# Float32 weights on SyncE's queue with a cast on chip, more chunks singly through the FFN, fewer transposes on TensorE

## The chip, the cores and the metric

One Trainium2 chip; the kernel runs on one of its cores. A core has TensorE (PE, matrix multiply, with its weight loads shown apart as PEld), VectorE (DVE), ScalarE (ACT), GpSimd (POOL) and SyncE (SP, which here only issues transfers), and 16 DMA engines that all queues share. The metric is the device time of one execution in microseconds (us).

## The reference

The kernel is a linear-attention layer followed by a feed-forward network (FFN). For each of 4 batches and 8 heads (head size 48) it walks 768 positions with a state of 48 x 48:

```
cur   = outer(u * k_t, v_t)
y_t   = r_t . (state + cur)
state = w * state + outer(k_t, v_t)
```

The 8 heads of y, side by side, make 384 columns; all batches make 3072 rows x. Then

```
h   = max(x @ w_in, 0)        # w_in  384 x 2048
out = (h * h) @ w_out         # w_out 2048 x 384
```

Inputs and output are float32; the kernel multiplies in bf16.

## The kernel before, in words

The 3072 positions are cut into 24 chunks of 128: chunk i is batch i % 4, block i // 4 of its 768 positions. Within a chunk the recurrence becomes matrix work; from block to block a state per batch is carried. The kernel's steps have short names, each with a number of its chunk, and one function `do_<name>` each:

- L: three loads of k, r, v of one chunk (192 KB each, in pieces of 192 bytes), on SP's queue (L482).
- kh, rt: k and r times powers of w, written as bf16 into `rk` (L496, L499). P0, P, du, dv: the term of u, as products, a row sum and a product (L503, L507, L511, L520). vb: v as bf16, on ACT (L525).
- Tk, Tr: transposes of kh and rt by TensorE (L531), evicted from PSUM as ek and er (L491 on ACT, L493 on DVE). From chunk PE_T on, T takes their place: one DMA transpose on SP's queue (L552).
- A, M: k times r (L562), masked on DVE (L576). Y: masked product times v, plus r times the state (L588, L593). U, S: the state's update (L603, L617, L618).
- xs: Y + dv (L611). X, xT: its transpose on TensorE (L624) and the copy to SBUF on ACT (L632).
- W1_q, W2_q: a quarter each of w_in and w_out, loaded on POOL's software queue, which casts float32 to bf16 on the way (L638, L643).
- F: a slice of the first FFN product into one PSUM bank (L652). R: relu on ACT (L665). Q: the square, on DVE (L674) or, for each fourth slice, on ACT (L672). G: a quarter of the second product (L684). os, st: eviction and store (L695, L699).

The FFN takes chunks singly or in pairs: `units()` makes the first SINGLE_HEAD and the last SINGLE_TAIL chunks single, the rest pairs. A single chunk has 4 F slices of 12 matmuls with 128 columns; a pair has 8 slices of 6 matmuls with 256.

The order on each engine isn't written out by hand. `Plan` holds every step with its possible engines, a cost on each, its needs and a priority (about a due time, one chunk each 6.25 us); `run()` places the steps one by one where they can start first, with a small model of the two DMA queues, and the instructions are issued in that order. Engines and SP's queue work in order: an instruction that waits holds all behind it. The model has room for 8 PSUM banks. `after` names a transfer's extra waits in the program: W1_q waits for v of chunk 1, W2_q for k or v of chunks 3 and 4. `OPEN` shifts the priorities of the first four chunks' steps, FLEX is the number of first chunks whose products may go to DVE as well as POOL, UB is the priority of u's row, SLACK adds time in the plan between a step and its reader, and LEAD places the loads of a chunk behind the T of an earlier one.

Of the kernel before, what the change touches and what calls it, by code (L numbers as in the profile page):

```python
# [8 lines left out]
FP32 = mybir.dt.float32  # L9
BF16 = mybir.dt.bfloat16  # L10
# [186 lines left out]
def make_plan():  # L197
    p = Plan()
    P = PERIOD
# [12 lines left out]
    all_units = units()  # L212
    unit_of = {i: n for n, chunks in enumerate(all_units) for i in chunks}

    def parts(n):
        return 4 * len(all_units[n])

    for i in range(N):
# [51 lines left out]
        p.add(f"xs{i}", "DVE", 0.47, [f"Y{i}", f"dv{i}"] + ([f"X{i-3}"] if i >= 3 else []), prio=t + 2.5,  # L270
              lat=0.65, give=[f"Y{i}"])
# [3 lines left out]
        p.add(f"X{i}", "PE", 0.17, [f"xs{i}"], prio=t + 3.0, lat=0.4, take=(f"X{i}", "A", 1), slack=SLACK[1] if i >= 4 else 0.0)  # L275
        p.add(f"xT{i}", "ACT", 0.38, [f"X{i}"] + ([f"F{n-4}_{parts(n-4)-1}"] if n >= 4 else []), prio=t + 3.0,
              lat=0.6, give=[f"X{i}"])
    for q in range(4):
        p.add(f"W1_{q}", "POOL", 0.85, W1GATE[q], prio=-60 + q, service=2.3)
        p.after[f"W1_{q}"] = W1GATE[q]  # L280
    for q in range(4):
        p.add(f"W2_{q}", "POOL", 0.85, W2GATE[q], prio=-55 + q, service=2.4)
        p.after[f"W2_{q}"] = W2GATE[q]
    for n, chunks in enumerate(all_units):
        i0, size = chunks[0], len(chunks)
        for s in range(parts(n)):
            t = (i0 / 2 + 1) * P + s * P / 8
            q = s // size
            p.add(f"F{n}_{s}", "PE", 0.66, [f"xT{i}" for i in chunks] + [f"W1_{q}"], prio=t, lat=0.95,
                  take=(f"H{n}_{s}", "H", 1))  # L290
            on_act = s % 4 == 3
            p.add(f"R{n}_{s}", "ACT", 0.49, [f"F{n}_{s}"], prio=t, lat=0.7,
                  give=[f"H{n}_{s}"] if on_act else [])
            p.add(f"Q{n}_{s}", "ACT" if on_act else "DVE", 0.53 if on_act else 0.6,
                  [f"R{n}_{s}"], prio=t + 0.7, lat=0.8, give=[] if on_act else [f"H{n}_{s}"],
                  ring=("hq", HQ, [f"G{i}_{q}" for i in chunks]))
        for j, i in enumerate(chunks):
            for q in range(4):
                t = (i0 / 2 + 2) * P + (4 * j + q) * P / 8
                p.add(f"G{i}_{q}", "PE", 0.65,  # L300
                      [f"Q{n}_{size*q+a}" for a in range(size)] + [f"W2_{q}"] + ([f"G{i}_{q-1}"] if q else []),
                      prio=t + 0.3, lat=0.95, take=(f"O{i}", "O", 1) if q == 0 else ())
# [7 lines left out]
def kernel(  # L310
# [11 lines left out]
    nc = tc.nc  # L322
# [13 lines left out]
    loads = ctx.enter_context(tc.tile_pool(name="loads", bufs=8))  # L336
    work = ctx.enter_context(tc.tile_pool(name="work", bufs=4))
    hid = ctx.enter_context(tc.tile_pool(name="hid", bufs=HQ))
    psum = ctx.enter_context(tc.tile_pool(name="psum", bufs=1, space=bass.MemoryType.PSUM))

    plan = make_plan()
# [284 lines left out]

    def do_xT(i):
        n = unit_of[i]
        j = all_units[n].index(i)
        if n not in xTs:  # L630
            xTs[n] = work.tile([128, CCH, GT], BF16, name=f"xT_{n}", tag="xT")
        nc.scalar.copy(xTs[n][:, :, L * j : L * (j + 1)], ps.pop(f"X{i}"))  # L632

    def do_W1(q):
        n = d_ff // 4
        t = const.tile([128, CCH, n], BF16, name=f"W1_{q}")
        W1[q] = t
        return nc.gpsimd.dma_start(out=t, in_=w_in_t[:, :, n * q : n * (q + 1)])  # L638

    def do_W2(q):  # L640
        t = const.tile([128, 4, d_model], BF16, name=f"W2_{q}")
        W2[q] = t
        return nc.gpsimd.dma_start(out=t, in_=w_out_t[:, 4 * q : 4 * q + 4, :])  # L643

    def do_F(n, s):
        size = len(all_units[n])
        per, wide = 4 // size, L * size
        hp = bank(f"H{n}_{s}").rearrange("p (a t) -> p a t", a=per)
        for fi in range(per):
            f = (per * s + fi) % 4  # L650
            for c in range(CCH):
                nc.tensor.matmul(  # L652
                    hp[:, fi, :],
                    W1[s // size][:, c, 128 * f : 128 * (f + 1)],
                    xTs[n][:, c, 0:wide],
                    start=(c == 0),
                    stop=(c == CCH - 1),
                    skip_group_check=True,
# [53 lines left out]
    for key in order:  # L712
        if key in plain:
            inst = plain[key]()
        elif key[:2] in ("W1", "W2"):
            inst = (do_W1 if key[1] == "1" else do_W2)(int(key[3:]))
        elif key[0] == "L":
            inst = do_L(key[1], int(key[2:]))
        elif "_" in key:
# [39 lines left out]
```

## Time and profile before

| | us |
|---|---|
| median of 3 runs (range) | 178.98 (178.73 to 179.65) |
| the profiled execution | 178.95 |
| its span, first to last instruction | 177.2 |
| PE busy | 165.6 (93%) |
| DVE busy | 132.2 (75%) |
| POOL busy | 110.3 (62%) |
| ACT busy | 107.0 (60%) |

Busy time counts an instruction from start to end. A matmul that waits for its operands, or whose neighbours do, looks long, so a busy PE early in the kernel isn't a PE at work all the time. The clock granted to TensorE was 0.997 of full speed. The DMA share is the mean over 16 engines and can go over 1, since packets of one engine overlap. Times in rows count from the start of the span.

### The profile page before, as it was taken

To read this page: it belongs to the slowest core of one execution; us is meant where nothing else is said; L and a number is where in the kernel's file an instruction comes from. 1 tells how busy PE (TensorE), PEld (TensorE's weight loads), DVE (VectorE), ACT (ScalarE), POOL (GpSimd) and SP (SyncE) were. 2 spreads that over 40 slices of the span, in tenths; PEclk is the share of its full clock that TensorE was granted. 3 is DMA by queue.
4 is the path that set the end of the run, shared out by engine and by line. 5 is a ranking of instruction groups with operands and counts; after the bars stand their busy time and mean duration, and the time that the engine had idled before them with its cause. 6 is when DMAs were issued, how large, how long until landed. Compare 5 with 4: busy or idle time off the path is not lost.

```text
span 177.2 us, 4677 instructions
## 1 busy us (share of the span) xinstructions
PE 165.6 (93%) x1852; PEld 126.6 (71%) x1852; DVE 132.2 (75%) x235; ACT 107.0 (60%) x208; POOL 110.3 (62%) x130
## 2 busy tenths in 40 slices
PE   2779789999999999999999999999999999999991
PEld 1249668787878886687786876877777777778750
DVE  4699999876789986499799879797796566544400
ACT  4444468747776766377386676576756654655622
POOL 5299416959988889999799968998694000000000
PEclk9999999999999999999999999999999999999998
DMA  3999999998999684879999999899794011110112
GB/s 75 202 177 200 191 185 185 186 210 160 202 203 218 174 159 83 158 150 253 185 175 213 117 216 225 174 227 197 149 183 128 0 48 44 44 41 7 44 46 89
DMA packets 97913, 26.25 MB, mean 148 GB/s; under 512 B 91234, under 2 KB 97892, under 8 KB 97892
## 3 DMA queue, kind: packets, MB, share of 16 engines
q1 hardware_dynamic: 94180, 22.82, 68.3%
q0 software_dynamic: 3712, 3.15, 11.1%
q8 instruction: 14, 0.23, 0.6%
q14 instruction: 7, 0.06, 0.1%
HBM read 20.45 MB, written 4.72 MB: 142 GB/s over the span
## 4 chain that ended last, share of the span: by engine, by line
PE 83%; DVE 9%; DMA 2%; issue 2%; SPq 1%; ACT 0%; DVEq 0%
PE ps_O L684 36%; PE ps_H L652 34%; PE ps_A L562 4%; PE ps_Y L593 2%; PE ps_X L624 2%; PE ps_Y L588 2%; DMA rf<-in_r_dram 2%; PE ps_U L603 2%; DVE dv L520 2%; DVE Bm L576 2%; DVE rk L499 1%; PE ps_Tr L531 1%; DVE hq L674 1%; DVE du L511 1%; PE ps_Tk L531 1%
## 5 line engine op out<-in xcount | busy, mean ns | idle before, releaser
L665 ACT ACTIVATE hr<-ps_H 128x512 bf16<-128x512 f32 x96 | 56.4, 598 | 34.5 <-PE ps_H L652 31.4
L652 PE MATMUL ps_H<-xT,W 128*128 128x128 bf16 (+1 forms) x768 | 76.1, 247 | 0.1
L684 PE MATMUL ps_O<-W,hq 128*128 128x384 bf16 x384 | 73.4, 326 | 0.0
L652 PEld LDWEIGHTS <-W 128*128 128x128 bf16 x768 | 59.1, 98 | 8.8 <-issue 0.2
L674 DVE TENSOR_TENSOR hq<-hr,ps_H 128x512 bf16<-128x512 bf16 x72 | 47.1, 681 | 13.3 <-ACT hr L665 13.3
L684 PEld LDWEIGHTS <-hq 128*128 128x128 bf16 x384 | 35.2, 98 | 17.3
L576 DVE TENSOR_TENSOR Bm<-ps_A,maskJT 128x512 bf16<-128x512 f32 x48 | 30.8, 683 | 12.2 <-PE ps_A L562 12.1
L496 POOL TENSOR_TENSOR rk<-kf,Wkhat 128x384 bf16<-128x384 f32 x23 | 23.6, 1024 | 8.1 <-DMA kf<-in_k_dram 6.9
L507 POOL TENSOR_TENSOR P<-P,ub 128x384 f32<-128x384 f32 x22 | 22.0, 1001 | 5.4 <-DVE P L503 5.2
L499 POOL TENSOR_TENSOR rk<-rf,Wt 128x384 bf16<-128x384 f32 x21 | 21.0, 1001 | 3.8 <-ACT hr L665 2.4
L503 POOL TENSOR_TENSOR P<-rf,kf 128x384 f32<-128x384 f32 x22 | 22.3, 1014 | 0.0
L520 POOL TENSOR_TENSOR dv<-vf,du 128x384 f32<-128x384 f32 x20 | 16.6, 830 | 6.9 <-DVE du L511 5.8
L632 ACT COPY xT<-ps_X 128x384 bf16<-128x384 bf16 x24 | 11.5, 478 | 10.3 <-PE ps_X L624 10.3
L525 ACT CAST vb<-vf 128x384 bf16<-128x384 f32 x24 | 12.2, 510 | 7.0 <-DMA vf<-in_v_dram 7.0
L672 ACT ACTIVATE hq<-hr 128x512 bf16<-128x512 bf16 x24 | 15.3, 635 | 0.1
L611 DVE TENSOR_TENSOR xs<-ps_Y,dv 128x384 bf16<-128x384 f32 x24 | 13.3, 552 | 1.9 <-PE ps_Y L593 1.8
L695 ACT COPY os<-ps_O 128x384 f32<-128x384 f32 x24 | 11.4, 477 | 4.4 <-PE ps_O L684 4.1
L511 DVE TENSOR_REDUCE du<-P 128x8 f32<-128x384 f32 x24 | 13.0, 544 | 0.7 <-POOL P L507 0.7
L593 PE MATMUL ps_Y<-vb,Bm 128*128 128x48 bf16 x192 | 11.9, 186 | 0.2
L618 DVE TENSOR_TENSOR S0W<-ps_U,WLm 128x384 bf16<-128x384 f32 x20 | 11.0, 556 | 0.6
L593 PEld LDWEIGHTS <-Bm 128*128 128x128 bf16 x192 | 10.0, 98 | 1.5 <-DVE Bm L576 0.5
L562 PE MATMUL ps_A<-rkT 48*128 48x128 bf16 x192 | 10.2, 229 | 0.7 <-ACT rkT L491 0.7
(52 smaller groups left out, 116.3 us busy)
## 6 DMA issues: line engine op xcount, KB each, us to landing
kf<-in_k_dram SPq DMA_DIRECT2D x24, 192.0 KB, 4.5
rf<-in_r_dram SPq DMA_DIRECT2D x24, 192.0 KB, 4.5
vf<-in_v_dram SPq DMA_DIRECT2D x24, 192.0 KB, 4.6
out_dram<-os SPq DMA_DIRECT2D x24, 192.0 KB, 2.5
W<-in_moe_w_in_dram POOLq DMA_DIRECT2D x4, 384.0 KB, 9.3
W<-in_moe_w_out_dram POOLq DMA_DIRECT2D x4, 384.0 KB, 8.3
rkT<-rk SPq DMA_TRANSPOSE x15, 3.4
wrow<-in_w_dram SPq DMA_DIRECT2D x1, 1.5 KB
```

The costliest lines, as they stand in the source:

```text
L496: engine(f"kh{i}").tensor_mul(rk_buf[i % NK][:, 1, :, 0:D], nat["k", i], Wkhat)
L499: engine(f"rt{i}").tensor_mul(rk_buf[i % NK][:, 0, :, 0:D], nat["r", i], Wt2)
L503: engine(f"P0{i}").tensor_mul(P0, nat["r", i], nat["k", i])
L507: engine(f"P{i}").tensor_mul(P0s[i], P0s[i], ub)
L520: engine(f"dv{i}").tensor_mul(dv, nat["v", i], du_b)
L562: nc.tensor.matmul(Ap[e][:, hc, :], rkT[p0 : p0 + D, HP + hc, :], rkT[p0 : p0 + D, hc, :], start=True, stop=True, skip_group_check=True,)
L576: nc.vector.tensor_mul(Bm[:, e], Ap[e], mask_b)
L593: nc.tensor.matmul(Y[:, hc, D * e : D * (e + 1)], Bm[:, e, hc, :], vb[:, 2 * hc + e, :], start=(c == 0), stop=True, skip_group_check=True,)
L652: nc.tensor.matmul(hp[:, fi, :], W1[s // size][:, c, 128 * f : 128 * (f + 1)], xTs[n][:, c, 0:wide], start=(c == 0), stop=(c == CCH - 1), ...
L665: nc.scalar.activation(hr, hp, AF.Relu)
L674: nc.vector.tensor_mul(hq, hr, hp)
L684: nc.tensor.matmul(ps[f"O{i}"][:, 0:d_model], hsq[n, f // per][:, f % per, L * j : L * (j + 1)], W2[q][:, f % 4, :], start=(f == 0), stop= ...
```

## The change

Constants:

```diff
-PE_T = 9
+PE_T = 6
-SINGLE_HEAD = 8
-SINGLE_TAIL = 0
+SINGLE_HEAD = 10
+SINGLE_TAIL = 2
-FLEX = 4
-UB = -94.95
-ST_SLACK = 3.0
+FLEX = 5
+UB = -94.75
+ST_SLACK = 2.0
-W2GATE = [["Lk3"], ["Lk3"], ["Lv3"], ["Lv4"]]
-LEAD = 3
-SLACK = (2.5, 0.5)
-LGATE = {}
-OPEN = {"kh": 8, "rt": -3, "P0": 8, "P": -3, "du": 0.0, "dv": 0.0, "S": 0.0}
+W2GATE = [["Lv3"], ["Lk4"], ["Lv4"], ["Lk5"]]
+HW1 = (0, 1, 2, 3)
+HW2 = (0, 1, 2)
+W1PRIO = (-93.5, -93.45, -92.4, -92.35)
+W2PRIO = (-91.5, -91.4, -91.3, -91.2)
+CASTS = ("ACT", "POOL")
+XD = 24
+WF = 5
+LEAD = 2
+SLACK = (1.0, 0.6, 0.5)
+LGATE = {6: ["W2_2"], 7: ["W2_3"]}
+OPEN = {"kh": 0, "rt": 12, "P0": -6, "P": 2, "du": 8, "dv": 0, "S": 2}
```

All four quarters of w_in and the first three of w_out are loaded as float32 by SP's queue into one of WF = 5 staging tiles, between the loads of the first chunks (loads of chunk i have priority -95 + i there), and a new step C casts each on ACT or POOL, whichever the plan finds free first. F and G wait for C instead of W. The last quarter of w_out stays on POOL's queue, and waits for k of chunk 5. The loads of chunk 6 wait in the program for W2_2, those of chunk 7 for W2_3. With XD = 24 no chunk takes the new path by which xT could be a DMA transpose.

```diff
+        for q in range(4):
+            if q in hw:
+                p.add(f"W{a}_{q}", "SP", 0.7, prio=prios[q], service=hw_time, ring=("wf", WF, [f"C{a}_{q}"]))
+                p.add(f"C{a}_{q}", CASTS, {e: {"ACT": 1.33, "POOL": 1.9, "DVE": 1.6}[e] for e in CASTS},
+                      [f"W{a}_{q}"], prio=-30 + q)
+            else:
+                p.add(f"W{a}_{q}", "POOL", 0.85, gates[q], prio=-60 + q, service=sw_time)
+                p.after[f"W{a}_{q}"] = gates[q]
...
+    def do_W(a, q):
+        part, shape = w_of[a](q)
+        if plan.eng[f"W{a}_{q}"] == "SP":
+            Wf[a, q] = stage.tile(shape, FP32, name=f"Wf{a}_{q}", tag="Wf")
+            return nc.sync.dma_start(out=Wf[a, q], in_=part)
+        Wb[a][q] = const.tile(shape, BF16, name=f"W{a}_{q}")
+        return nc.gpsimd.dma_start(out=Wb[a][q], in_=part)
+
+    def do_C(a, q):
+        f = Wf.pop((a, q))
+        Wb[a][q] = const.tile(list(f.shape), BF16, name=f"W{a}_{q}")
+        copy(f"C{a}_{q}", Wb[a][q], f)
```

xT is laid out chunk by chunk, so that a pair's F reads two blocks of 128 columns instead of 256 in a row:

```diff
-            xTs[n] = work.tile([128, CCH, GT], BF16, name=f"xT_{n}", tag="xT")
-        nc.scalar.copy(xTs[n][:, :, L * j : L * (j + 1)], ps.pop(f"X{i}"))
+            xTs[n] = work.tile([128, size, CCH, L], BF16, name=f"xT_{n}", tag="xT", padded_shape=[None, 2, None, None])
+        nc.scalar.copy(xTs[n][:, j], ps.pop(f"X{i}"))
...
-                    xTs[n][:, c, 0:wide],
+                    xTs[n][:, :, c, :],
```

More of the change, by code (lines that the diff above doesn't have):

```diff
@@ L274, in make_plan, with ready_of @@
                   lat=1.2 if c else 0.65, give=[f"U{i}"])
[L275 to L283, printed above, removed]
+        room = [f"F{n-4}_{parts(n-4)-1}"] if n >= 4 else []
+        if i < XD:
+            p.add(f"X{i}", "PE", 0.17, [f"xs{i}"], prio=t + 3.0, lat=0.4, take=(f"X{i}", "A", 1),
+                  slack=SLACK[1] if i >= 4 else 0.0)
+            p.add(f"xT{i}", "ACT", 0.38, [f"X{i}"] + room, prio=t + 3.0, lat=0.6, give=[f"X{i}"])
+        else:
+            p.add(f"xT{i}", "SP", 0.9, [f"xs{i}"] + room, prio=t + 3.0, service=0.6, slack=SLACK[2])
+    for a, hw, gates, prios, hw_time, sw_time in (
+        (1, HW1, W1GATE, W1PRIO, 2.05, 2.3), (2, HW2, W2GATE, W2PRIO, 2.1, 2.4)
+    ):
+        for q in range(4):
[3 more added lines that the diff above has]
+                      [f"W{a}_{q}"], prio=-30 + q)
+            else:
+                p.add(f"W{a}_{q}", "POOL", 0.85, gates[q], prio=-60 + q, service=sw_time)
+                p.after[f"W{a}_{q}"] = gates[q]
+    def ready_of(a, q):
+        return f"C{a}_{q}" if q in (HW1 if a == 1 else HW2) else f"W{a}_{q}"
     for n, chunks in enumerate(all_units):
@@ L288, in make_plan @@
             q = s // size
[L289 removed]
+            p.add(f"F{n}_{s}", "PE", 0.66, [f"xT{i}" for i in chunks] + [ready_of(1, q)], prio=t, lat=0.95,
                   take=(f"H{n}_{s}", "H", 1))
```

31 lines of the change are left out of this document (16 added, 15 removed).

## The prediction

> **What bounds the kernel now.** I read the page's slices first, then busy time by stretch, then the head in order of time.
>
> ```profile
> span 177.2 us, 4677 instructions
> PE   2779789999999999999999999999999999999991
> DVE  4699999876789986499799879797796566544400
> DMA  3999999998999684879999999899794011110112
> ```
>
> ```profile
> 3.54:16.66 13.12, 10.62 (x74) 7.24 (x75) 10.57 (x18) 5.34 (x12) 8.57 (x9) 1.00 1.18 190
> 16.66:26.36 9.70, 7.88 (x122) 6.86 (x118) 9.65 (x16) 5.07 (x10) 3.61 (x5) 1.00 1.23 188
> 28.16:173.40 145.24, 145.24 (x1634) 110.72 (x1631) 108.44 (x191) 92.76 (x183) 95.60 (x103) 1.00 0.76 145
> 173.40:177.30 3.90, 0.07 (x1) 0.00 (x0) 0.00 (x0) 0.48 (x1) 0.00 (x0) 0.87 0.28 101
> ```
>
> In the second fence a row gives a stretch, its length, then busy time (and instructions) of PE, weight loads, DVE, ACT and POOL, the clock, the DMA share and GB/s. From 28.16 to 173.40 us TensorE has no gap: 145.24 of 145.24 us. After it come 3.8 us of last eviction and store. So the span is a head of 28.2 us, a solid block, and a tail, and an edit pays in two ways only: it takes matmul work out of the block, or it gets more of that work done before the block begins. A third way loses: a supplier of the block comes so late that a gap opens. In the head TensorE looks 80% busy, but 74 instructions in 10.62 us are matmuls stretched by waiting; the full engines there are DVE (9.65 of 9.70 us) and the DMA (share 1.18 to 1.23, about 190 GB/s, against 0.76 later).
>
> ```profile
> 5.85 0.56 DVE L503 TENSOR_TENSOR P<-rf,kf 128x384 f32<-128x384 f32 x1 [2.92 <-DMA rf<-in_r_dram]
> 7.94 1.19 POOL L496 TENSOR_TENSOR rk<-kf,Wkhat 128x384 bf16<-128x384 f32 x1 [4.81 <-DMA kf<-in_k_dram]
> 10.13 3.24 POOL L638 DMA_DIRECT2D W<-in_moe_w_in_dram  x4
> 10.43 0.55 DVE L520 TENSOR_TENSOR dv<-vf,du 128x384 f32<-128x384 f32 x1
> 12.98 0.51 ACT L525 CAST vb<-vf 128x384 bf16<-128x384 f32 x1 [1.19 <-DMA vf<-in_v_dram]
> 15.74 0.48 ACT L632 COPY xT<-ps_X 128x384 bf16<-128x384 bf16 x1 [0.26 <-PE ps_X L624]
> 15.77 0.99 POOL L507 TENSOR_TENSOR P<-P,ub 128x384 f32<-128x384 f32 x1
> 15.93 1.25 DVE L520 TENSOR_TENSOR dv<-vf,du 128x384 f32<-128x384 f32 x1
> 16.70 1.45 PE L652 MATMUL ps_H<-xT,W 128*128 128x128 bf16 x12
> 20.44 0.48 ACT L632 COPY xT<-ps_X 128x384 bf16<-128x384 bf16 x1 [1.65 <-PE ps_X L624]
> 22.47 0.67 PEld L652 LDWEIGHTS <-W 128*128 128x128 bf16 x12 [0.17 <-DMA W<-in_moe_w_in_dram]
> 26.74 0.48 ACT L632 COPY xT<-ps_X 128x384 bf16<-128x384 bf16 x1 [0.21 <-PE ps_X L624]
> 28.16 0.81 PE L684 MATMUL ps_O<-W,hq 128*128 128x384 bf16 x4
> ```
>
> In order of time (start, length, engine; in brackets the wait before it and who ended it): k of chunk 1 has landed by 7.94, v of chunk 2 by 12.98, five loads later, so one load lands each 1.01 us. xT of chunks 0, 1, 2 is written at 16.2, 20.9, 27.2; F starts at 16.70, waits at 22.47 for the third slice of W_in, and the first G runs at 28.16.
>
> **The change, part by part.** (1) PE_T 9 to 6, SINGLE_HEAD 10, SINGLE_TAIL 2: matmul work.
>
> ```profile
> 39.77 0.23 PE ps_Tk L531 x4
> 42.30 0.65 PE ps_O L684 x4
> 43.83 0.67 PE ps_H L652 x12
> 74.60 0.66 PE ps_H L652 x6
> 98.91 1.31 PE ps_H L652 x12
> rkT<-rk SPq DMA_TRANSPOSE x15, 3.4
> ```
>
> Three chunks lose Tk and Tr: 6 x 0.23 = 1.38 us of TensorE, inside the block (their six evictions on ACT and DVE go too; neither is full there). Four chunks go singly: a single F slice (12 matmuls) takes 0.67, a pair's (6) 1.31 / 2 = 0.655. Four slices of 0.67 against eight half-shared of 0.655 is 2.68 against 2.62 a chunk, so 4 x 0.06 = +0.24. G is unchanged. Sum: **-1.14 us**. Singles in the tail shorten nothing, as the block runs to the last G; the last eviction and store stay. T of chunks 6, 7, 8 becomes three DMA transposes, each 3.4 us from issue to landing, behind kh and rt; SP is in order, so the loads and stores planned behind a T wait with it. I cost that at nothing: those loads are prefetch for chunks 8 to 11, whose F begins with the first six-matmul slice at 74.60. If that cover fails, one late transpose is up to 3.4 us.
>
> (2) Weights on SP's queue. The price of a float32 slice (786 KB) is not shown, so it is bounded.
>
> ```profile
> q0 software_dynamic: 3712, 3.15, 11.1%
> 140.00:160.00 20.00, 20.00 (x201) 14.75 (x199) 10.93 (x18) 12.01 (x24) 0.00 (x0) 1.00 0.12 41
> 5.00:30.00 25.00, 20.68 (x246) 16.41 (x245) 23.87 (x39) 13.84 (x27) 13.92 (x15) 1.00 1.22 192
> ```
>
> A slice on the software queue takes 0.111 x 177.2 / 8 = 2.46 us of all 16 engines. Stores alone (140 to 160 us) move 41 GB/s at share 0.12, so 340 GB/s when full: 786 KB in 2.3 us. At the head's 192 GB/s, which small load packets set, it would be 4.1. The store is the nearer row (1.5 KB runs against 2 KB), and the head's share of 1.22 means overlap, 2.3 / 1.22 = 1.9; I take 2.1, ends 1.9 and 4.1. Order on SP's queue: chunks 0 and 1, W_in slices 0, 1, chunk 2, W_in 2, 3, chunk 3, W_out 0 to 2, chunk 4, 5. v of chunk 1 lands at 7.94 + 2 x 1.01 = 9.96; W_in then at 12.1, 14.2, chunk 2 at 17.2, W_in at 19.3, 21.4, chunk 3 at 24.4, W_out at 26.5, 28.6, 30.7, chunk 4 at 33.8, chunk 5 at 36.8. u's row moves behind chunk 0's loads, about two loads later; P, du and dv of chunk 0 are not needed until xs, so I cost it at nothing, at most 1.5 (the bu matmuls) if Tk waits behind it.
>
> ```profile
> L525 ACT CAST vb<-vf 128x384 bf16<-128x384 f32 x24 | 12.2, 510 | 7.0 <-DMA vf<-in_v_dram 7.0
> L632 ACT COPY xT<-ps_X 128x384 bf16<-128x384 bf16 x24 | 11.5, 478 | 10.3 <-PE ps_X L624 10.3
> L491 ACT COPY rkT<-ps_Tk 128x512 bf16<-128x512 bf16 x7 | 4.1, 585 | 5.0 <-PE ps_Tk L531 5.0
> L405 POOL MEMSET rk<- 128x256 bf16 x4 | 1.1, 311 | 0.0
> L499 POOL TENSOR_TENSOR rk<-rf,Wt 128x384 bf16<-128x384 f32 x21 | 21.0, 1001 | 3.8 <-ACT hr L665 2.4 <-DMA rf<-in_r_dram 1.4
> ```
>
> Seven casts of 128x1536. On ACT 128 more columns cost 585 - 478 = 107 ns, so 510 + 9 x 107 = 1.47 us. On POOL between 6 x 0.311 = 1.9 (memset, one stream) and 4 x 1.001 = 4.0 (two inputs). All on ACT: 10.3 us, into the 25 - 13.84 = 11.2 us that ACT idles from 5 to 30 us. Weights ready: W_in 13.6, 15.7, 20.8, 22.9; W_out 28.0, 30.1, 32.2.
>
> The Trainium skill, page "DMA: Bandwidth & Descriptors", section "Rules for kernel authors", says to issue a DMA that casts from GpSimd, where the conversion rides on the transfer; by that rule the seven passes are pure loss, up to 10.3 us of engine time. Page "GPSIMD Engine Reference", section 4.1, puts GpSimd near line rate on one-input work, which would place the POOL cast near the low end above; no row here shows one.
>
> (3) POOL is freed of seven issues, 7 x 0.81 = 5.7 us (3.24 / 4 each), and FLEX 5 lets DVE share chunk 4. DVE's dv takes 0.55 us at 10.43 and 1.25 at 15.93, where POOL's P (15.77) runs beside it: five 1.0 us products that POOL now has time for take 2.8 to 6 us off the full DVE. OPEN reorders the first four chunks' products; its worth lies between the terms here, so I give it none of its own.
>
> (4) What the head gains. The F matmuls alone, before the first G:
>
> ```profile
> 0.00:28.16 28.16, 7.75 (x108) 6.88 (x108) 1.00 1.09 172
> ```
>
> That is 108 / 12 = 9 slices. With xT at about 15, 19.5 and 25 (DVE relieved by 1.2, 1.4, 2.2) and the weights above, slices 0 and 1 of chunks 0 and 1 run from 15 to 21, their slices 2 and 3 until 24.2, and chunk 2's four from 25 to 27.7: 12 slices by 28, then G. Three more slices are 3 x 0.67 = 2.0 us done ahead of the block. Ends: 0, if DVE is not relieved; 2.8, if chunk 3's A and transposes (0.8) also fit. I take **-2.0**.
>
> ```profile
> 30.00 0.99 POOL L496 TENSOR_TENSOR rk<-kf,Wkhat 128x384 bf16<-128x384 f32 x1 [0.35 <-DMA kf<-in_k_dram]
> 36.26 0.40 PE L562 MATMUL ps_A<-rkT 48*128 48x128 bf16 x8
> 43.66 0.83 PE L652 MATMUL ps_H<-xT,W 128*128 128x128 bf16 x12
> DMA to landing us min/median/max: 6.0/6.0/6.0
> ```
>
> (5) Who then is late. k of chunk 4 landed at 30.0 and comes at about 31.8; its rk products end at 32 and its A ran at 36.26, so 1.8 us vanish in 4 us of slack, and G's left over fill the rest. The last W_out slice stays on POOL, issued once k of chunk 5 is in (about 34.8): with the 6.0 us from issue to landing of the same slice before, about 41 against 39.2. Until then 12 G steps (four chunks, three quarters) and chunk 3's F can run: 12 x 0.65 + 2.68 = 10.5 us, for the 13 us from 28, the rest attention. Tight; I cost it 0, up to 2. Loads of chunk 6 and 7 wait on SP for W_out 2 and 3; behind them stand only later loads, T6 and stores that need the same slice. LEAD 2, SLACK, ST_SLACK and the new xT layout: 0, covered by ready G's; with none ready, an A that the cut SLACK lets come 1.5 us sooner (2.5 to 1.0) waits out 1.5 us at most.
>
> Sum: 178.95 (the profiled execution; the median shown is 178.98) - 1.14 - 2.0 = **175.8 us**.
>
> **Rivals.** *Only the matmul work (chance 0.20).* The weights' bytes share the same full DMA engines, so the first G comes no earlier (W_out 0 ready at 28.0 against 28.16) and the head keeps its 28.2 us: 178.95 - 1.14 = 177.8. For it: the DMA share of 1.22; against: DVE is full too, and it is relieved. The Trainium skill, page "DMA: Bandwidth & Descriptors", section "Issuing engines are not separate DMA queues", holds that transfers from any issuer interleave on the same 16 engines and that another issuer saves issue time alone; by it this rival is the outcome.
>
> *Slower: ACT's order (0.20).* A cast that waits for its landing holds vb, xT and hr behind it. ACT has 11.2 us free in the head and the casts take 10.3, so 0.9 us of waiting is free; from there each microsecond is a microsecond of hr, and so of F. If each of the seven waits half a load, 0.5 us, that is 3.5 - 0.9 = 2.6 late in place of the gain: 178.95 - 1.14 + 2.6 = 180.4. For it: casts stand in an order fixed beforehand, and slices at 4.1 us would do it; against: POOL can take some.
>
> *More (0.10).* Slices at 1.9 us bring W_out forward by 7 x 0.2 = 1.4 us, on top of the 2.8 end: 178.95 - 1.14 - 2.8 - 0.7 (half, as xT then limits) = 174.3.
>
> **How the numbers follow.** Forecast 0.50 (own range 174.8 to 177.2), only the work 0.20, slower 0.20, more 0.10. Half a per cent, 0.9 us, is about what can be told from no change. The work-only case straddles that bound, 0.14 faster and 0.06 same; of the slower case 0.03 is same. Faster 0.74, same 0.09, slower 0.17. The range takes half of the outer cases on each side, and the 2 us of the late last slice: 173.7 to 180.2.
>
> **What would show it.** Right: F starts near 15, first G near 28 with about 12 F slices before it; DVE products near 0.55 rather than 1.2 us; TensorE's block of matmuls without gaps, some 1.1 us less work in it; W_in landing 2.1 us apart. Wrong: ACT idle on the landing of a float32 slice with hr late; TensorE gaps at 33 to 41 us waiting for the last W_out slice; gaps at 45 to 60 us on rkT from the DMA; slices 4 us apart.

## The result and the profile after

| | before | after |
|---|---|---|
| median (range) of the timed runs, us | 179.31 (178.73 to 179.65) | 186.82 (186.10 to 187.36) |
| the profiled execution, us | 178.95 | 186.41 |
| its span, us | 177.2 | 184.7 |
| granted clock of TensorE | 0.997 | 0.980 |

The changed kernel takes 1.042 times as long, 95% interval 1.0366 to 1.0474. The forecast was 175.8 us and its range ended at 180.2: wrong in sign and outside the range.

The page after the change (four of its lines; the strips cut the span into 40 slices of 4.6 us, in tenths):

```profile
span 184.7 us, 4818 instructions
PE   2789999942999999999999999999999999999991
POOL 4137120494086849599697978959689561000000
PEclk9999999997599999999999999999999999999999
```

TensorE, solid from 28 us in the kernel before, has a hole in the ninth and tenth slice, and its clock drops right behind it. GpSimd is full in the ninth. Busy time by stretch (columns as in the prediction: PE, weight loads, DVE, ACT, POOL, clock, DMA share, GB/s) shows the place:

```profile
30.00:34.00 4.00, 3.86 (x35) 2.35 (x34) 3.46 (x7) 4.00 (x6) 0.00 (x0) 1.00 0.99 195
34.00:38.00 4.00, 3.95 (x59) 3.35 (x59) 3.58 (x5) 4.00 (x9) 3.08 (x3) 1.00 1.25 203
38.00:42.00 4.00, 1.05 (x7) 0.51 (x6) 4.00 (x1) 1.12 (x3) 4.00 (x6) 1.00 1.22 188
42.00:46.00 4.00, 1.07 (x9) 0.91 (x9) 4.00 (x5) 0.46 (x1) 1.84 (x2) 0.78 0.49 97
46.00:50.00 4.00, 4.00 (x41) 3.07 (x39) 2.48 (x6) 0.72 (x2) 0.00 (x0) 0.50 0.74 121
50.00:54.00 4.00, 4.00 (x43) 2.83 (x40) 2.43 (x5) 2.85 (x6) 2.65 (x3) 0.87 0.11 39
```

From 38 to 42 us VectorE is busy for all 4.00 us with one instruction (x1), and TensorE has 1.05 us of work. Instruction by instruction (start, length, engine, line; in brackets the wait before it), first TensorE, then VectorE, then GpSimd:

```profile
44.91 0.59 PE L552 MATMUL ps_Tk<-identity,rk 128*128 128x128 bf16 x4 [5.86 <-DVE Bm L597]
```

```profile
36.70 7.56 DVE L541 TENSOR_TENSOR dv<-vf,du 128x384 f32<-128x384 f32 x1
44.19 1.27 DVE L597 TENSOR_TENSOR Bm<-ps_A,maskJT 128x512 bf16<-128x512 f32 x2
```

```profile
36.20 0.92 POOL L671 DMA_DIRECT2D W<-in_moe_w_out_dram  x1 [0.72 <-DMA kf<-in_k_dram]
37.15 1.01 POOL L517 TENSOR_TENSOR rk<-kf,Wkhat 128x384 bf16<-128x384 f32 x1
...
42.86 0.98 POOL L524 TENSOR_TENSOR P<-rf,kf 128x384 f32<-128x384 f32 x1
```

So dv of chunk 4, which FLEX 5 put on VectorE, took 7.56 us where the prediction's row has 0.55. It started while GpSimd issued the last quarter of w_out, and ended at 44.26, 0.42 us after the last of the seven products that GpSimd ran back to back from 37.15 to 43.84. M of chunk 4 (Bm) stood behind it; TensorE waited 5.86 us for that, and came back to a clock of 0.50.

To sum this up I use TensorE's *lateness*: the start of a matmul minus the price of all matmuls before it, each priced by its columns at the rate of the prediction's G and F rows (0.65 / 4 us for 384 columns, 0.67 / 12 for 128, other widths on the straight line through these two; the few float32 ones at the start count four times, in every kernel alike). All matmuls together cost 158.2 us before and 157.1 after. Lateness in us, near these times:

| kernel | 28 us | 37 us | 45 us | 53 us | end |
|---|---|---|---|---|---|
| before | 14.8 | 14.8 | 14.8 | 14.9 | 15.1 |
| after | 13.8 | 14.6 | 20.5 | 23.4 | 23.6 |

In these two profiles the head is 1.0 us ahead at 28 us; 0.8 of it is lost again by 37. The gap cost 5.9, and the slow clock behind it 2.9 more. Over the whole span: 23.6 - 15.1 - 1.1 = +7.4, and the two profiled executions differ by 7.46.

### The profile page after: what moved, and what is told of

It is laid out like the page before. It is cut to its first block, busy times and chain, and to the rows that moved or that the text cites. A ratio compares the mean times of both kernels' runs of the same rounds, so it can differ in the third digit from the quotient of the medians.

```text
span 184.7 us, 4818 instructions
## 1 busy us (share of the span) xinstructions
PE 168.4 (91%) x1924; PEld 129.4 (70%) x1924; DVE 138.1 (75%) x235; ACT 115.9 (63%) x214; POOL 100.3 (54%) x118
## 4 chain that ended last, share of the span: by engine, by line
PE 76%; DVE 7%; ACT 6%; DMA 4%; SPq 3%; issue 1%; POOL 1%
PE ps_O L717 32%; PE ps_H L685 32%; DVE dv L541 4%; DMA kf<-in_k_dram 4%; PE ps_A L583 4%; ACT hr L698 3%; ACT W L512 2%; PE ps_Y L614 2%; PE ps_Y L609 2%; SPq L503 2%; PE ps_X L645 2%; PE ps_U L624 2%; DVE Bm L597 1%; SPq L669 1%; POOL rk L517 1%
## 5 line engine op out<-in xcount | busy, mean ns | idle before, releaser
L685 PE MATMUL ps_H<-xT,W 128*128 128x128 bf16 (+1 forms) x864 | 77.6, 241 | 0.5 <-ACT xT L657 0.3
L717 PE MATMUL ps_O<-W,hq 128*128 128x384 bf16 x384 | 74.8, 329 | 0.2
L685 PEld LDWEIGHTS <-W 128*128 128x128 bf16 x864 | 62.2, 100 | 8.4 <-issue 0.5
L707 DVE TENSOR_TENSOR hq<-hr,ps_H 128x512 bf16<-128x512 bf16 x72 | 47.6, 680 | 16.5 <-ACT hr L698 16.2
L517 POOL TENSOR_TENSOR rk<-kf,Wkhat 128x384 bf16<-128x384 f32 x20 | 20.3, 1016 | 14.7 <-DMA kf<-in_k_dram 12.1
L541 POOL TENSOR_TENSOR dv<-vf,du 128x384 f32<-128x384 f32 x20 | 16.6, 830 | 19.6 <-DVE du L532 17.7
L524 POOL TENSOR_TENSOR P<-rf,kf 128x384 f32<-128x384 f32 x21 | 21.3, 1013 | 9.4 <-DMA rf<-in_r_dram 9.4
L520 POOL TENSOR_TENSOR rk<-rf,Wt 128x384 bf16<-128x384 f32 x22 | 22.1, 1003 | 7.0 <-DMA rf<-in_r_dram 7.0
L528 POOL TENSOR_TENSOR P<-P,ub 128x384 f32<-128x384 f32 x20 | 20.2, 1008 | 0.9 <-DVE P L524 0.6
L512 ACT CAST W<-Wf 128x1536 bf16<-128x1536 f32 x7 | 10.5, 1502 | 0.9 <-DMA Wf<-in_moe_w_in_dram 0.9
```

Of the source, the lines that this page charges most:

```text
L517: engine(f"kh{i}").tensor_mul(rk_buf[i % NK][:, 1, :, 0:D], nat["k", i], Wkhat)
L520: engine(f"rt{i}").tensor_mul(rk_buf[i % NK][:, 0, :, 0:D], nat["r", i], Wt2)
L524: engine(f"P0{i}").tensor_mul(P0, nat["r", i], nat["k", i])
L528: engine(f"P{i}").tensor_mul(P0s[i], P0s[i], ub)
L541: engine(f"dv{i}").tensor_mul(dv, nat["v", i], du_b)
L685: nc.tensor.matmul(hp[:, fi, :], W1[s // size][:, c, 128 * f : 128 * (f + 1)], xTs[n][:, :, c, :], start=(c == 0), stop=(c == CCH - 1), sk ...
```

## The experiments

Lines in the traces of experiments can stand a few higher than in the changed kernel. "Before" was run beside each kernel on the same chip, with medians of 178.5 to 179.2 us. Letters in the expectations: theory A holds that a VectorE product with both inputs in SBUF is kept out by any unbroken row of GpSimd products; C that the later loads and the cut slack are to blame, and C2 that a product is kept out only if it arrives while GpSimd is issuing a transfer; E that after such an issue the row of products keeps VectorE out until GpSimd really pauses; F that the waits of the loads of chunks 6 and 7 cost the second part. Where an expectation names another, its own words say what it holds.

### Is it that product?

Two ways to take it from VectorE: only its engine, with the order of all instructions kept, or FLEX 4, planned anew.

```diff
     order = plan.run()
+    plan.eng["dv4"] = "POOL"      # e1_dv4_pool
```

> The changed kernel with one instruction moved: dv of chunk 4, which took 7.56 us on VectorE beside an unbroken row of GpSimd products, is issued on GpSimd; the order is kept. Theory A (that VectorE product with two SBUF inputs is held until GpSimd pauses, and TensorE's 5.9 us gap and its slow clock follow from it): no VectorE instruction over 1.4 us, no TensorE gap over 1 us, the granted clock at 1.00 in every slice, 177 to 178 us. Theory B (the last quarter of w_out, landing at 43.1, starves TensorE whatever the product does): TensorE still stands from 39 to 43, 182 to 185 us.

```diff
-FLEX = 5
+FLEX = 4                          # e2_flex4
```

> The changed kernel with FLEX = 4, planned anew: chunk 4's products all go to GpSimd, as before the change. Theory A: 176.5 to 178.5 us, no VectorE product over 1.4 us. Theory B: over 182, with the gap before the last quarter of w_out lands.

Measured: 181.80 us, ratio 1.0125 (1.0044 to 1.0206), and 181.19 us, ratio 1.0127 (1.0073 to 1.0181). In both the gap of 5.86 us is gone and the clock is back (0.998 and 0.996). That one instruction is thus worth about 5 us of the 7.5, and some 2.3 us (0.0127 x 178.9) are left over.

### What kept the product out?

The same product put on VectorE in the kernel before, where GpSimd has a row of products beside it but no transfer at the head of that row:

```diff
     order = plan.run()            # kernel before
+    plan.eng["dv4"] = "DVE"       # e3_before_dv4_dve
```

> The kernel before with the same single instruction the other way: dv of chunk 4 on VectorE, the order kept, everything else as it was. Theory A: GpSimd has some six products with no wait between them from 38.5, so that dv takes 4 to 7 us, TensorE gets a gap and the time is 182 to 187. Theory B: it takes at most 1.3 us, as the other contended products of before did, and the time stays within 0.5 us of before.

VectorE's row for it:

```profile
40.03 0.88 DVE L521 TENSOR_TENSOR dv<-vf,du 128x384 f32<-128x384 f32 x1
```

Measured: 180.02 us in one run, within what runs of before took beside it (178.25 to 181.55). The product waited out one GpSimd operation and got in. A plain row of products is not enough: theory A falls in this form.

The same trace holds a second case, which was not planned: dv of chunk 3. GpSimd, then VectorE:

```profile
29.73 0.81 POOL L644 DMA_DIRECT2D W<-in_moe_w_out_dram  x1
...
32.48 0.99 POOL L504 TENSOR_TENSOR P<-rf,kf 128x384 f32<-128x384 f32 x1
```

```profile
32.29 1.60 DVE L521 TENSOR_TENSOR dv<-vf,du 128x384 f32<-128x384 f32 x1
```

Here a transfer's issue stands at the head of an unbroken row of three products. VectorE came in the second of them, was kept out through the third as well, and ended at 33.89, 0.42 us after the row, while GpSimd issued its next transfer.

Three operations whose results nothing uses, added behind M of chunks 7, 8 and 9 in the kernel before (a float32 copy, a product, a row sum):

```diff
+        if i in (7, 8, 9):
+            ...
+            if i == 7:
+                nc.vector.tensor_copy(probe, ub)
+            elif i == 8:
+                nc.vector.tensor_mul(probe, ub, ...)
+            else:
+                nc.vector.tensor_reduce(probe[:, :, 0], ub, ...)
```

> The kernel before with one extra VectorE instruction behind the mask step of chunks 7, 8 and 9, where GpSimd is busy without gaps: a float32 SBUF copy (7), a float32 product of two SBUF tiles (8), a sum over one SBUF tile (9); nothing else changes and their results are not used. Theory A, in the form that only an instruction with two SBUF inputs is held: copy 0.4 to 0.6 us, product 2 to 6 us, sum 0.54 us. If the copy is held too, it is any instruction that reads SBUF at the full rate. Theory B: product at most 1.3 us.

```profile
56.06 0.97 DVE L581 COPY probe<-ub 128x384 f32<-128x384 f32 x1
```

```profile
62.26 1.17 DVE L583 TENSOR_TENSOR probe<-ub,WLm 128x384 f32<-128x384 f32 x1
```

Measured: 178.85 us in one run. Copy and product each wait for one GpSimd operation (0.97 and 1.17 us), the row sum does not (0.55).

The issue of the last w_out quarter moved, in the changed kernel: first by its gate only (v of chunk 4 in place of k of chunk 5; the order kept), then to right behind the loads of k of chunk 4:

```diff
     order = plan.run()
+    plan.after["W2_3"] = ["Lv4"]  # e8_gate_earlier
```

> The changed kernel, order and engines kept (dv of chunk 4 on VectorE), but the last quarter of w_out waits for v of chunk 4 instead of k of chunk 5, so that GpSimd issues it some 0.7 us earlier and is in a product, not in the issue, when dv of chunk 4 arrives at 36.7. Theory C2 (a VectorE product is overtaken for a whole row of GpSimd products only if it arrives during GpSimd's transfer issue): dv takes 0.55 to 1.6 us, no long TensorE gap, 179 to 182 us. Theory D2 (any unbroken row of GpSimd products does it, the other runs were luck): dv takes 5 us or more, 185 to 188.

```profile
36.19 0.92 POOL L672 DMA_DIRECT2D W<-in_moe_w_out_dram  x1
37.13 1.01 POOL L518 TENSOR_TENSOR rk<-kf,Wkhat 128x384 bf16<-128x384 f32 x1
38.09 1.00 POOL L521 TENSOR_TENSOR rk<-rf,Wt 128x384 bf16<-128x384 f32 x1
39.04 0.99 POOL L525 TENSOR_TENSOR P<-rf,kf 128x384 f32<-128x384 f32 x1
```

```profile
37.45 3.02 DVE L542 TENSOR_TENSOR dv<-vf,du 128x384 f32<-128x384 f32 x1
```

Measured: 181.72 us, ratio 1.0168 (1.0106 to 1.0231). The issue hardly moved (36.19), but the product now arrived at 37.45, after the issue, inside the first product. It was kept out all the same, to 40.47, 0.44 us after GpSimd's third product, where GpSimd paused. So C2 falls: it need not arrive during the issue. A fourth run, which the ratio leaves out, took 185.59 us at a clock of 0.981, much as the changed kernel does; it has no trace.

```diff
     order = plan.run()
+    plan.after["W2_3"] = ["Lv3"]  # e13_issue_moved
+    order.remove("W2_3")
+    order.insert(order.index("Lk4") + 1, "W2_3")
```

> The changed kernel, dv of chunk 4 on VectorE, engines and order kept but for one transfer: GpSimd issues the last quarter of w_out ten microseconds sooner, in its pause before 34 us, so that no issue lies ahead of the row of products beside dv. Theory E: dv of chunk 4 takes 0.55 to 1.5 us, no TensorE gap over 1 us, 179 to 181.5. If the row of products alone does it: 3 us or more, as in the changed kernel and in e8.

GpSimd, then VectorE:

```profile
25.09 0.92 POOL L674 DMA_DIRECT2D W<-in_moe_w_out_dram  x1 [6.76 <-DMA vf<-in_v_dram]
...
38.28 1.00 POOL L520 TENSOR_TENSOR rk<-kf,Wkhat 128x384 bf16<-128x384 f32 x1 [0.57 <-DMA kf<-in_k_dram]
39.33 1.22 POOL L523 TENSOR_TENSOR rk<-rf,Wt 128x384 bf16<-128x384 f32 x1
```

```profile
38.93 0.77 DVE L544 TENSOR_TENSOR dv<-vf,du 128x384 f32<-128x384 f32 x1
```

Measured: 181.01 us, ratio 1.0122 (1.0090 to 1.0154). The product is on VectorE as in the changed kernel, beside a GpSimd row as full, but the issue lies 13 us back, with a long pause in between: 0.77 us instead of 7.56. (In eight of the ten runs the clock was 0.986 to 0.990, in the profiled one 1.00; a shorter stall in those, which have no trace, is not excluded.)

Then the same thing made on purpose, in the kernel before: at P0 of chunks 9, 12 and 15 four extra GpSimd products and one VectorE product with both inputs in SBUF, their results unused; at 12 and 15 GpSimd also issues a small transfer first (and at 15 the first extra product has to wait for a result of ScalarE).

```diff
+        if i in (9, 12, 15):
+            ...
+            if i != 9:
+                ...
+                nc.gpsimd.dma_start(out=scr, in_=w_out_t[:, 0:1, :])
+            nc.vector.tensor_mul(got, P0, ub)
+            for n in range(4):
+                ...
+                nc.gpsimd.tensor_mul(x, vbs[i - 1] if i == 15 and n == 0 else Wt2, ub)
```

> The kernel before with extra work beside chunks 9, 12 and 15: behind P0 GpSimd runs four extra float32 products, and VectorE one product of two SBUF tiles that can start when P0 ends. At chunk 9 nothing else; at 12 and 15 GpSimd first issues a small casting transfer, and at 15 the first extra product also waits for ScalarE. Results are not used; only the length of VectorE's product counts, not the time. Theory E (after GpSimd has issued a transfer, products behind it without a pause keep VectorE's product out until they pause): 1.0 to 1.6 us at 9; 4 to 6 us at 12; if a wait ahead of the first product is such a pause, 1.0 to 2.5 us at 15, else as at 12. If the issue plays no part, all three are alike.

GpSimd at chunk 9 and at chunk 12:

```profile
59.31 4.18 POOL L513 TENSOR_TENSOR x<-Wt,ub 128x384 f32<-128x384 f32 x4
```

```profile
77.28 0.60 POOL L509 DMA_DIRECT2D scr<-in_moe_w_out_dram  x1
77.91 3.84 POOL L513 TENSOR_TENSOR x<-Wt,ub 128x384 f32<-128x384 f32 x4
81.71 0.82 POOL L529 TENSOR_TENSOR dv<-vf,du 128x384 f32<-128x384 f32 x1
```

The VectorE product at chunks 9, 12 and 15:

```profile
61.10 0.57 DVE L510 TENSOR_TENSOR got<-P,ub 128x384 f32<-128x384 f32 x1
```

```profile
77.37 5.58 DVE L510 TENSOR_TENSOR got<-P,ub 128x384 f32<-128x384 f32 x1 [1.12 <-POOL P L503]
```

```profile
97.36 4.96 DVE L510 TENSOR_TENSOR got<-P,ub 128x384 f32<-128x384 f32 x1
```

Measured: 191.74 us in one run, with two TensorE waits of 5.6 and 4.2 us. The same four GpSimd products let the VectorE product in when no transfer stood ahead of them (0.57 us), and kept it out for 5.58 and 4.96 us when one did, until 0.4 us after the row's end at 82.53 and 101.90. At chunk 15 ScalarE's result was there already, so whether such a wait would let VectorE in was not tried. With the changed kernel, the gate experiment and dv of chunk 3 above, theory E is seen five times. What GpSimd does differently after an issue is not visible in a trace; only that it does.

The rule is not complete, though. The kernel before has one case that goes against it (GpSimd, then VectorE; the issues are those of 10.13 to 13.37 us in the prediction's rows):

```profile
13.39 1.35 POOL L496 TENSOR_TENSOR rk<-kf,Wkhat 128x384 bf16<-128x384 f32 x1
```

```profile
12.56 1.32 DVE L499 TENSOR_TENSOR rk<-rf,Wt 128x384 bf16<-128x384 f32 x1
```

This product came as GpSimd began the last of four issues, with two products right behind them, and was done at 13.88: 0.51 us after the issues' end, before GpSimd's first product (which took 1.35 us), not after the row. At the same place it took 1.18 to 1.26 us in e10, e3 and e4, and 0.54 in e9. What tells this case from the five, the four issues in a row or another thing, no run here tests.

The Trainium skill, page "SBUF — State Buffer", section "Who interferes with whom", says that a VectorE instruction with two SBUF inputs and a GpSimd one that reads SBUF exclude each other, whoever issues first, for the whole instruction. The waits of one operation (0.88, 1.17 us) agree with it. The 7.56 us go beyond it: VectorE waited there for seven products, all of which are recorded as starting after it.

### What are the other 2.3 us?

Starting from FLEX 4. First, slack and lead of the kernel before:

```diff
-LEAD = 2
-SLACK = (1.0, 0.6, 0.5)
+LEAD = 3
+SLACK = (2.5, 0.6, 0.5)           # e5_lead3
```

> e2 (the changed kernel with FLEX 4) with LEAD back at 3 and the slack behind a DMA transpose back at 2.5. In e2 TensorE loses 2.4 us in small steps between 86 and 143 us, where k of a chunk is used as it lands and rkT lands 0 to 4 us ahead of A. Theory C (the loads planned one chunk later leave no margin): that loss goes, 178.4 to 179.2 us median. Theory D (single chunks, or ACT, make it): 180.5 to 181.5 as e2.

Measured: 181.92 us, ratio 1.0166 (1.0087 to 1.0245): no better. Theory C falls.

Then the whole new loading of weights taken back, and, apart from that, only the waits of the loads of chunks 6 and 7:

```diff
-W2GATE = [["Lv3"], ["Lk4"], ["Lv4"], ["Lk5"]]
-HW1 = (0, 1, 2, 3)
-HW2 = (0, 1, 2)
-LGATE = {6: ["W2_2"], 7: ["W2_3"]}
+W2GATE = [["Lk3"], ["Lk3"], ["Lv3"], ["Lv4"]]
+HW1 = ()
+HW2 = ()
+LGATE = {}                        # e7_weights_back
```

> e2 with the weights back on GpSimd's queue with the cast in flight, gated as before the change; no staging, no casts on ACT. If the float32 path gains in the head (as the changed kernel's profile hints: 1.0 us less TensorE idle by 29 us than before), this is 0.5 to 1.5 us slower than e2, 181.7 to 182.7. If the seven casts on ACT and the later loads of chunks 2 to 4 cost more than the queue gives, it is 0.5 to 2 us faster than e2, 179.2 to 180.7.

```diff
-LGATE = {6: ["W2_2"], 7: ["W2_3"]}
+LGATE = {}                        # e14_no_lgate
```

> e2 with LGATE empty: the loads of chunks 6 and 7 no longer wait on SP for the third and fourth quarter of w_out (4.7 us in e2, the loads of chunk 7 issued at 43.5). The prediction costed that wait at nothing. Theory F (it starves the chain of chunks 7 to 9 and so drains the ready work from which TensorE fills its waits): 179 to 180.2, and the small TensorE waits after 85 us go. If it was free: 180.7 to 181.7, as e2.

Measured: 179.48 us, ratio 1.0031 (0.9993 to 1.0069), and 178.55 us, ratio 0.9995 (0.9956 to 1.0034). Weights back or waits away, most or all of the 2.3 us go either way. In the FLEX 4 kernel SyncE had stood at the load of chunk 7 for the last quarter (the DMA queue's own waits: total, times, longest):

```profile
SPq L503 <- DMA W<-in_moe_w_out_dram: 4.7, 1, 4.7
```

That looked like theory F proven. But the plan knows those waits too and orders other engines' work around them, so the edit had changed two things. Two more kernels were to part them, beside a repeat of e14:

```diff
     order = plan.run()            # of e14: e18_wait_only
+    for lw in "krv":
+        plan.after[f"L{lw}6"] = ["W2_2"]
+        plan.after[f"L{lw}7"] = ["W2_3"]
...
     order = plan.run()            # of e2: e19_order_only
+    for lw in "krv":
+        del plan.after[f"L{lw}6"], plan.after[f"L{lw}7"]
```

> e14's order of instructions on every engine, with the waits of the loads of chunks 6 and 7 for w_out's third and last quarter put into the program again. If the wait itself costs what separates FLEX 4 with the waits (181.2) from the same without (178.55): 180.3 to 181.5, SyncE held 4 to 5 us at k of chunk 7 and small TensorE waits after 85 us. If the planned order around it does: 178.2 to 179.2.

> FLEX 4 with the order of instructions that the plan writes when it counts the waits of the loads of chunks 6 and 7, but without those waits in the program. If the wait itself costs the difference: 178.2 to 179.3. If the order does: 180.3 to 181.5, with TensorE waits after 85 us as before.

> The kernel of e14 unchanged, on the chip of these two runs, so that the three stand beside each other: 178.0 to 179.2 by its first runs, ratio to before 0.9956 to 1.0034.

Measured on one chip: 179.78 us, ratio 1.0013 (0.9970 to 1.0055); 181.52 us, ratio 1.0128 (1.0042 to 1.0213); 180.07 us, ratio 1.0070 (1.0025 to 1.0114). The first is hardly a test of the wait: in that order k and r of chunk 7 stand ahead of the last quarter, so their waits fall away, and v's held SyncE for under 0.2 us (44.69 to 44.87); it is nearly a repeat. The second decides. There k of chunk 7 is issued with no wait (SyncE's queue):

```profile
39.41 2.20 SPq L505 DMA_DIRECT2D kf<-in_k_dram  x1
```

and the time is that of FLEX 4 with the wait (1.0128 against 1.0127). Taking the wait alone out of the program brings nothing measurable, and F's 178.2 to 179.3 us are missed, so theory F falls in this form. What is left is the order planned around it: three measurements of the other order gave 0.9995, 1.0013 and 1.0070. On the last chip the intervals overlap, so the size, 0.6 to 1.3%, is loose, and that chip alone doesn't prove a difference. TensorE's waits after 46 us, with FLEX 4 (total, times, longest):

```profile
PE ps_X L645 <- DVE xs L632: 0.7, 1, 0.7
PE ps_A L583 <- ACT hr L698: 0.7, 1, 0.7
PE ps_A L583 <- DMA rkT<-rk: 0.2, 1, 0.2
```

e19 has the first two as well (0.7 and 0.6), e14 has none of them; the rest is lateness in the head, below. Which step's place in the order makes them was not tried.

### Who gives the head's gain back?

Lateness again, with waits that TensorE shows:

| kernel | 28 us | 37 us | 45 us | 53 us | end |
|---|---|---|---|---|---|
| e14 | 13.4 | 14.3 | 15.3 | 15.3 | 15.5 |
| e14 again (e20) | 13.9 | 15.0 | 15.8 | 15.8 | 16.4 |
| e2 (FLEX 4) | 14.4 | 15.2 | 15.5 | 15.5 | 18.0 |
| e19 | 14.8 | 16.2 | 16.9 | 16.9 | 19.0 |
| e7 (weights back) | 15.7 | 15.8 | 15.8 | 15.8 | 16.5 |

In e14 TensorE is 1.4 us ahead of before at 28 us and 0.5 behind it at 45. The loss in between is steady: the six traces of FLEX 4 with the new loading (e2, e5, e14, e18, e19, e20) lose 1.1 to 2.6 us there, the four of the kernel before with nothing changed ahead of 28 us (before, e3, e4, e9) 0.0 to 0.3, and e7, with the weights back, 0.1. The gain ahead of it is not steady. These four stand at 13.8 to 15.6 us at 28 us (mean 14.6), and the nine of the new loading in the changed order (the six, the changed kernel, e1 and e8) at 13.4 to 14.8 (mean 14.2). Mean against mean the head gains 0.4 us, less than either kind scatters, so the 1.0 and 1.4 us of single traces can't be told from chance. TensorE's waits from 28 to 60 us in e14:

```profile
PE ps_O L717 <- DMA W<-in_moe_w_out_dram: 0.8, 1, 0.8
PE ps_O L717 <- ACT W L512: 0.3, 1, 0.3
```

The last quarter landed at 43.2, and a cast on ScalarE was late. Three edits of e14: the last quarter on SyncE too, or issued by GpSimd once v of chunk 3 is in, or all casts on GpSimd.

```diff
-HW2 = (0, 1, 2)
+HW2 = (0, 1, 2, 3)                # e15_last_quarter_sp
-W2GATE = [["Lv3"], ["Lk4"], ["Lv4"], ["Lk5"]]
+W2GATE = [["Lv3"], ["Lk4"], ["Lv4"], ["Lv3"]]   # e16_last_quarter_early
-CASTS = ("ACT", "POOL")
+CASTS = ("POOL",)                 # e17_casts_pool
```

> Beside e14 (FLEX 4, no waits of the loads of chunks 6 and 7; 178.55 us), the last quarter of w_out is also loaded as float32 by SP's queue and cast on ScalarE. If the late last quarter (landed 43.20 in e14, TensorE waiting 0.77 us) is what gives the head's gain back: it lands before 40, the gap is gone, and the time is 177.0 to 178.0. If ScalarE's casts give it back: an eighth cast of 1.50 us makes it worse, 179 to 180.5.

> Beside e14, GpSimd issues the last quarter of w_out once v of chunk 3 has landed, so in its pause of 24.8 to 34 us, and not behind k of chunk 5. If the late last quarter gives the gain back: it lands before 38, the gap at 43 is gone, 177.0 to 178.0. If ScalarE's casts do: no change, 178.3 to 178.8. Its 786 KB then share the engines with the float32 slices 0 to 2 of w_out, which may make these later by up to 2.1 us: then 179 to 180.

> Beside e14, all seven casts are on GpSimd and none on ScalarE. If ScalarE's casts (7 x 1.50 us, ScalarE full from 26 to 38 us) give the gain back: TensorE's idle time at 45 us is below 14.5 us and the time 177 to 178. If not, GpSimd's casts, 1.9 to 4.0 us each by the prediction's bounds, push its products later: 179 to 182. Either way it measures the price of the cast on GpSimd, and of the VectorE products beside it.

Measured: 179.48 us, ratio 1.0049 (1.0015 to 1.0084); 181.09 us, ratio 1.0101 (1.0008 to 1.0194); 181.31 us, ratio 1.0142 (1.0097 to 1.0187). None is faster; each moves the wait. In e15 the last quarter lands at 36.7 and the wait at 43 is gone (lateness 15.3 at 37 us, 15.6 at 53), but a new one stands at 116 us:

```profile
116.63 1.47 PE L685 MATMUL ps_H<-xT,W 128*128 128x256 bf16 x12 [0.81 <-ACT hr L698]
```

In e16 the quarter lands at 35.5, the two slices before it land 2.0 us later than in e14 (28.8 and 30.9 against 26.8 and 28.9), and TensorE waits 2.2 us for casts. In e17 the casts take GpSimd no longer than ScalarE (min/median/max ns, first and last start):

```profile
L514 POOL CAST W<-Wf x7: 1462/1467/1662, 12.0 to 32.3; 128x1536 bf16<-128x1536 f32 x7
```

but its products come later, and TensorE waits 1.1 us each for xs, for rk and for xT. So e14 loses in two steps of about equal size: 0.9 us from 28 to 37 us, of which 0.3 shows as the wait for a cast and the rest has no name here, and 1.0 us from 37 to 45, of which 0.8 is the wait for the last quarter. No rearrangement tried here avoids both.

### The transposes by themselves

In the kernel before, PE_T 6 alone, and in e7, PE_T back to 9:

```diff
-PE_T = 9
+PE_T = 6                          # kernel before: e10_before_pet6
-PE_T = 6
+PE_T = 9                          # e7: e11_before_pet9_head
```

> The kernel before with one constant of the change: PE_T = 6, so that chunks 6, 7, 8 are transposed by DMA. By the prediction's own term six groups of four matmuls at 0.23 us leave the block: 177.6 us, 1.3 below before. If the three transposes on SP's queue hold the loads behind them, 179 or more.

> e7 (the change without the float32 path and without FLEX 5) with PE_T back at 9: what is left of the change are ten and two single chunks, OPEN, LEAD, SLACK, the xT layout. e10 showed PE_T = 6 alone at +1.2 us on the kernel before. If that holds here, 178.0 to 178.8, below e7 by 0.7 to 1.5 and at or below before. If the matmul work decides, 1.3 above e7: 180.8.

Measured: 179.96 us, ratio 1.0067 (1.0033 to 1.0100), and 180.31 us, ratio 1.0066 (1.0024 to 1.0107). Alone, PE_T 6 takes 1.3 us of matmuls out and makes the kernel 1.2 us slower: lateness at the end is 17.5 against 15.1, with new waits in the block (two places of TensorE's order of time), neither of them for a DMA transpose:

```profile
61.19 0.49 PE L652 MATMUL ps_H<-xT,W 128*128 128x128 bf16 x6 [0.57 <-ACT xT L632]
```

```profile
81.04 0.70 PE L652 MATMUL ps_H<-xT,W 128*128 128x256 bf16 x5 [0.49 <-ACT hr L665]
```

With the change's other settings it seems worth a little: e7 has 1.0031 with 6, 1.0066 with 9, and the intervals overlap. No kernel here beats the one before.

## Why the prediction was wrong, by its own steps

**Part 3, FLEX 5: the step that failed.** It said that FLEX 5 lets VectorE share chunk 4, gave this no price of its own, and took from VectorE's two rows, 0.55 us free and 1.25 beside a GpSimd product, that this is the whole range of such a product. The relief that it counted on came another way, too. Five products were to leave VectorE, worth 2.8 to 6 us; it ran 12 of these two-input products before and 17 after, four of them chunk 4's. In chunks 0 to 3 it was relieved all the same, with 7.7 us for 13 products where 12 took 10.0: two of them met GpSimd at work and took over 0.6 us, where five had before, for GpSimd was busy for 7.35 us from 5 to 30 us and not for 13.92. The lengths of VectorE's dv after the change (min/median/max ns):

```profile
L541 DVE TENSOR_TENSOR dv<-vf,du x4: 547/559/7557, 12.0 to 36.7; 128x384 f32<-128x384 f32 x4
```

Three of four were as predicted, the fourth fourteen times as long. The bound held for a collision with one GpSimd operation. The one product of before with which VectorE meets GpSimd's issues with products right behind them (12.56) took 1.32 us, so that trace could not give this price. But the change itself left one issue on GpSimd by part (2), gated on chunk 5's k, just where FLEX 5 put new two-input work on VectorE; the prediction treated the two edits apart.

**The gap's price.** It followed M and not dv's own reader: dv is needed only at xs, but M of chunk 4 stood behind it on VectorE, in order. What is queued behind a late instruction was asked for SyncE's queue and for ScalarE, and not for VectorE. And the idle time had a second price, the clock: 5.86 us of gap were followed by windows at 0.78, 0.50 and 0.87, another 2.9 us. The Trainium skill, page "TensorE: Matmul & The Clock Gate", part 1, has the clock halve after an idle stretch; the 0.50 of 46 to 50 us agrees, and the prediction had priced a gap at its length alone.

**Part 1, -1.14 us: right as work, not as time.** All matmuls together went from 158.2 to 157.1 us. But in the kernel before PE_T 6 alone cost 1.2 us. Whether the cover that it named for T on SyncE's queue failed there stays open: the new waits are for xT and hr, and none shows for rkT.

**Part 2: sizes right, the head's order partly wrong.** The first two slices of w_out landed at 27.5 and 29.6, the 2.1 us apart that was taken between 1.9 and 4.1; the last two of w_in at 19.6 and 22.3, 2.7 apart. The cast took 1.50 against 1.47, and all seven went to ScalarE, as costed:

```profile
L512 ACT CAST W<-Wf 128x1536 bf16<-128x1536 f32 x7 | 10.5, 1502 | 0.9 <-DMA Wf<-in_moe_w_in_dram 0.9
```

Both bounds for GpSimd's cast (1.9 and 4.0 us) were too high: 1.47 in the experiment. u's row, costed at nothing and at most 1.5, cost 1.14:

```profile
6.33 1.64 PE L459 MATMUL ps_bu<-urow,ones 1*128 1x384 f32 x2 [1.14 <-DMA urow<-in_u_dram]
```

SyncE's issue was not free either, in either kernel. It took 4.03 us over v of chunk 3 (before, up to 5.46 us over one load), and the DMA share fell to 0.82 from 22 to 24 us:

```profile
18.00 4.03 SPq L503 DMA_DIRECT2D vf<-in_v_dram  x1
```

The slices of w_out came 1.0 us after the forecast, chunk 4 landed at 33.2 (k) where 31.8 was expected, and GpSimd, freed of seven issues, idled 9.36 us up to 34.19:

```profile
34.19 1.30 POOL L524 TENSOR_TENSOR P<-rf,kf 128x384 f32<-128x384 f32 x1 [9.36 <-DMA rf<-in_r_dram]
```

Behind that pause came the issue and then the seven products of chunks 4 and 5 in one row.

**Part 4, -2.0 us: half of it at most.** F began at 16.61 (15 expected) and the first G ran at 29.75 (28), with the 12 slices ahead of it that were forecast; F's busy time and instructions up to there:

```profile
0.00:29.75 29.75, 10.57 (x144) 9.56 (x144) 1.00 1.00 256
```

By lateness that is 1.0 us gained, 1.4 in e14, and 0.4 as the mean over all traces with each head. The relief of VectorE that the term rested on did come, 2.3 us over chunks 0 to 3, if by another way than part 3's.

**Part 5, "tight; I cost it 0, up to 2": the bound was the truth.** The last quarter landed at 43.1, not 41, and in e14 costs 0.77 us; with what is lost from 28 to 37 us it takes back what part 4 gained. The loads of chunks 6 and 7 costed at nothing: right for the wait itself, which held SyncE for 4.7 us and cost nothing measurable; what is left is the order which the plan wrote around them, 0.6 to 1.3% slower as measured.

**The rivals.** "Slower: ACT's order" had the sign, with 180.4 us, by another mechanism: ScalarE was full from 30 to 38 us (4.00 of 4.00 twice in the windows above), but the late casts show as waits of a few tenths, not 2.6. "Only the matmul work" is, in the end, nearest to the change with its fault taken out: the head's gain is small and does not last. But its work term does not come through either: e14 measured 0.9995, 1.0070 when repeated, and 1.0013 in its near twin, where the work alone would give 0.994.

## What to carry to other kernels

An operation moved to VectorE with both inputs in SBUF is at risk behind a transfer issued by GpSimd that is followed by a full row of GpSimd products; look for the two together, in the order of both engines, and ask what stands behind that operation on VectorE. A short operation's price is not bounded by its collisions in a quiet place. A gain of half a microsecond in the head can't be read from one trace against one other; compare all the traces that share the head. And when an option feeds a planner as well as the program, keep the order and change the wait, or keep the wait out and keep the order, before either is blamed.

## What the runs showed of the hardware

- A VectorE product with two SBUF inputs normally waits for one GpSimd product and gets in (0.88, 1.17 us); behind a GpSimd transfer issue it stayed out until the row of products ended: 7.56, 3.02, 5.58, 4.96 and 1.60 us, each ending 0.4 us after the row's last product. It makes no difference whether it arrives during the issue (36.70, 77.37) or after it (37.45, 97.36, 32.29), and with the issue 13 us back it was 0.77. One case goes the other way: during the last of four issues in a row it got in 0.51 us behind them, ahead of the products (12.56 in the kernel before).
- A float32 copy from SBUF on VectorE waits for GpSimd as well (0.97 us); a row sum does not (0.55).
- GpSimd casts 128x1536 from float32 to bf16 in 1.47 us, as fast as ScalarE (1.50).
- A stall hides later ones. The changed kernel shows no TensorE wait after 45 us; with the same order but for the moved issue, and the stall gone, the dv4 experiment and the moved issue wait 1.1 and 0.9 us for xT near 138 us, and end 3.9 and 5.5 us less late, not 8.8. Part of the difference lies ahead of the stall: these two were 0.9 and 2.1 us later already at 28 us. So here the price read from the stall was more than its removal brought.
